# Eleven power matrices of a state-space scan: from VectorE, between the value steps, to GpSimd, in a row

## The chip, the cores and the metric

One core of a Trainium2 chip. The metric is the device time of one execution in microseconds (us). Three runs of the kernel before took 151.14, 151.69 and 152.08 us; the median is 151.69. The kernel has two parts that share the core, called A and B, and its output is their results side by side.

## The reference

Part A is a diagonal complex recurrence over 2,048 steps with 448 states, read in and out by complex matrices. Part B is attention of 16 heads in which each position looks at 8 positions, 2 apart.

```python
def _A_ref(x, Lambda_re, Lambda_im, B_re, B_im, C_re, C_im, log_dt, Dskip):
    ...
    Lam_bar = jnp.exp(dt * Lam)
    B_bar = ((Lam_bar - 1.0) / Lam)[:, None] * Bmat
    Bu = jnp.einsum("bld,pd->blp", x + 0j, B_bar)
    for t in range(L):
        h = Lam_bar[None, :] * h + Bu[:, t, :]
        hs.append(h)
    ...
    y = 2.0 * jnp.einsum("blp,dp->bld", hseq, Cmat).real + x * Dskip[None, None, :]

def _B_ref(x, wqkv, wo):
    ...
    idx = pos[:, None] - off[None, :]        # off = 0, 2, ..., 14
    logits = jnp.einsum("bhsd,bhswd->bhsw", q, kg) * scale
    attn = _softmax(jnp.where(mask[None, None, :, :], logits, -1e9), axis=-1)
    o = jnp.einsum("bhsw,bhswd->bhsd", attn, vg)
    return (...)(o, 0, 2, 1, 3).reshape(B, S, D) @ wo
```

## The kernel before

**Part B.** Projections (`proj_t`, `proj`) run on TensorE; VectorE multiplies queries with shifted keys (`qk`, L295 and L299), and TensorE sums these products into logits. `softmax` works on one half of each 16 positions at a time: `softmax(1)` the later half, `softmax(0)` the earlier one. It turns the logits (L330), takes their maxima on VectorE (L332), subtracts them on TensorE (L337), takes the exponential on ScalarE into a tile `e` (L339), sums on TensorE (L345), and normalises on VectorE (L348, L349). `pv` makes the values: for each of the 8 offsets VectorE multiplies weights by values (L389, 128x1792 bf16) and, from the second on, adds the product (L392, 128x1792). These are the value steps. There are four calls of `pv`: two for the later half, then two for the earlier one. A call's sum goes through a DMA transpose (L404), the output matrix on TensorE (L420), and out.

**Part A.** The recurrence is done in blocks. A power of the recurrence's factor acts on a block by a matrix product, so each power k has a "mat", a 128x1024 bf16 tile made by one multiplication of a pattern `Dm` with the power's rows of `Scat` (`mat`, L599). `Scat` is complete at about 15 us. There are thirteen: k = 1, 2, 3, 4, 8, 12, 16, 32, ..., 1024 (`KPOW`), and one more, `g`, of another shape. Who uses them:
- `level1` (L643, L647): blocks of four, with k = 1, in three groups of states, `mh` = 0, 1, 2.
- `scan` (L663 to L676): first k = 4, 8, 12, then seven steps with 16, 32, ..., 1024. Each step is a product on TensorE (L673) out of one of two buffers `pbuf`, and a copy on ScalarE (L676) into the other. The first 64 columns of these buffers must be zero; `alloc_h` clears them on GpSimd (L633).
- `ends` (L690, L692): the states G at the ends of the blocks, with k = 4, 8, 12.
- `correct` (L699, L700): with k = 1, 2, 3, a product of G on TensorE that VectorE adds to the other states (the corrections, 21 of them).
- `y` (L711 to L718): the output, sixteen pieces.

**Order.** The framework orders the instructions of each engine at build time: among those that are ready, the one emitted first goes first; after that an engine's queue is in order. Two kinds of edges are added by hand: `cx.chain` for TensorE, and `cx.order(ins, after, "NoSync")`, which puts an instruction behind another in its engine's order without a wait. `lanes` (projections) has GpSimd relays, memsets of one element (L130), whose last one is `cx.relay`; the last is done at 51.74 us. `alloc_h` puts its clearings behind it.

`mats_behind(keys, after)` makes mats and puts each behind the instruction `after`. In `body`, the mats of k = 1 and 4 go behind the maxima of the first softmax; the other eleven go through `put`, behind the value steps of the first two calls of `pv`, one or two to a gap. `pv` calls `between[w - 1]` behind its w-th addition. The same list holds the five steps of `softmax(0)`, named `fs`. `eng` in other functions chooses the engine of a copy.

The scan's buffers share memory with older tiles. `pbuf` of the first group uses the places of `e` and of the logits `lgs`, so their clearing has to wait until `softmax(0)` has read both.

Of the kernel before, what the change touches and what calls it, by code (L numbers as in the profile page):

```python
# [11 lines left out]
ALU = mybir.AluOpType  # L12
# [31 lines left out]
NPW = len(KPOW)  # L44
# [386 lines left out]
class PartA:  # L431
# [139 lines left out]
        for k in range(KT):  # L571
            nc.scalar.activation(self.Dg[:, k, :], ident[:], ACT.Copy, scale=dsk[:, k:k + 1])

    def mats_behind(self, keys, after):
        for i in keys:
            key = "g" if i == "g" else KPOW[i]
            self.cx.order(self.mat(key, self.Scat[:, NPW if i == "g" else i]), after, "NoSync")

    def rot_rows(self, re, im):
        V, Sg = self.nc.vector, self.Scat[:, NPW]  # L580
# [3 lines left out]
        V.tensor_scalar(Sg[PL:NCH, 1, 0:NM], re[PL:NCH], -1.0, None, op0=ALU.mult)  # L584
        return Sg

    def mat(self, key, scal):
        if key == "g":
            sh = [NCH, NM, 2, PL]
            t_ = self.pool.tile(sh, bf16, name="matg")  # L590
            in0 = self.Dm[:, :, 0].unsqueeze(1).unsqueeze(1).to_broadcast(sh)
            in1 = scal[:, :, 0:NM].rearrange("p h m -> p m h").unsqueeze(3).to_broadcast(sh)
            self.mats[key] = t_[:].rearrange("p m h q -> p m (h q)")
        else:
            sh = [NCH, 2, PL, MP]
            t_ = self.pool.tile(sh, bf16, name=f"mat{key}")
            in0, in1 = self.Dm[:].unsqueeze(1).to_broadcast(sh), scal.unsqueeze(2).to_broadcast(sh)
            self.mats[key] = t_[:].rearrange("p h q m -> p m (h q)")
        return self.nc.vector.tensor_tensor(t_[:], in0, in1, op=ALU.mult).ins  # L599

    def setup_b(self, eng):
        nc, cx = self.nc, self.cx
# [120 lines left out]
@with_exitstack  # L723
def body(ctx: ExitStack, tc: tile.TileContext, A_x, A_Lre, A_Lim, A_Bre, A_Bim, A_Cre, A_Cim, A_logdt, A_Dskip,
         B_x, B_wqkv, B_wo, out):
    nc = tc.nc
    pool = ctx.enter_context(tc.tile_pool(name="sb", bufs=1))
    psum = ctx.enter_context(tc.tile_pool(name="ps", bufs=1, space=bass.MemoryType.PSUM))
    out_v = out[0].rearrange("(p j) e -> p j e", j=T)
    cx = Ctx(tc, pool, psum)  # L730
    b = PartB(cx, B_x, B_wqkv, B_wo, out_v[:, :, D:2 * D])
    a = PartA(cx, A_x, A_Lre, A_Lim, A_Bre, A_Bim, A_Cre, A_Cim, A_logdt, A_Dskip, out[0].rearrange("(n b) e -> n b e", b=4)[:, :, 0:D])
    parts = ((512, 1024), (1024, 1536), (1536, 2048))
    b.alloc()
    b.load_xn(0, 2)
    b.load_w(D, 0, D, nc.scalar)
    a.load_params()
    b.load_xn(2, 4)
    cx.consts()
    a.consts()  # L740
    b.clear()
    nc.scalar.activation(cx.spot2[:], cx.wz[0:1, 0:1], ACT.Exp)
    b.load_w(0, D, D, nc.sync)
    for g in parts:
        b.load_x(*g)
    b.consts()
    b.load_w(2 * D, 2 * D, D, nc.sync)
    a.load_bc()
    a.load_x()
    b.zero_halo(b.vd)  # L750
    b.load_wo()
    a.load_c()
    a.load_d()
    cx.warm(8)
    turns = [lambda i=i: b.turn_x(i, "VA"[i % 2], ("pt", "lg")[i // 2]) for i in range(4)]
    for f in turns[:2]:
        for ins in f():
            cx.chain(ins)
    powers = a.params()
    cx.warm(2)  # L760

    def later():
        powers(b.turned)
        b.mix_w(a.reduced)
        a.params_g()
        return ()

    values = [b.proj(j, "A") for j in (*range(HJ, T), *range(HJ))]
    qk, soft = b.qk(0) + b.qk(1), {}
    weave = [(5, turns[2:] + [later])] + [(s_, [f]) for s_, f in zip(WEAVE, qk)]  # L770

    def turn():
        a.mats_behind(["g"], b.product)
        soft[1] = b.softmax(1)
        return soft[1][0][0]() + soft[1][0][1]()

    def prepare():
        a.mats_behind([0, 3], b.maxima)
        fs = mats_b[:1] + soft[1][0][4:] + mats_b[1:]
        return [ins for f in fs for ins in f()]  # L780

    mats_b = a.setup_b("A")
    weave += [(157, [turn])] + [(160 + 4 * i, [lambda i=i: soft[1][0][2 + i]()]) for i in range(2)] + [(200, [prepare])]
    cx.lanes([b.proj_t(t0, t1, g, "A") for t0, t1, gs in ((0, 256, (0, 1, 2)), (256, 512, (0, 1, 2)), (0, 512, (4, 5, 6, 3)))
              for g in gs]
             + [b.proj_t(*t, g, "A") for t in parts for g in (0, 1, 2, 4, 5, 6, 3)] + values, weave, 10)
    at1 = soft[1][1]
    b.halo(b.vd, 6, HALO)
    b.halo(b.vd, 0, 6)
    a.skip()  # L790
    fs, at0 = b.softmax(0)

    def put(*fs):
        return lambda after: [f() if callable(f) else a.mats_behind([f], after) for f in fs]

    wo = [b.pv(1, at1, 0, 4, between=[put(4, *fs[:2]), put(5, 6), put(*fs[2:4]), put(7, 8), put(fs[4]), put(9, 10)])]
    wo.append(b.pv(1, at1, 4, 8, between=[put(11, 12), put(), put(1, 2)]))
    a.alloc_h()
    for mh in range(3):
        a.level1(mh)  # L800
        a.scan(mh)
        if mh == 0:
            a.setup_c("A")
    wo[0]()
    for mh in range(3):
        a.ends(mh)
    for b_ in range(3):
        for mh in range(3):
            a.correct(b_, mh)
    wo[1]()  # L810
    wo.append(b.pv(0, at0, 0, 4))
    wo.append(b.pv(0, at0, 4, 8, True))
    for b_, r in itertools.product((3, 0, 1, 2), range(4)):
        ins = a.y(r, b_)
        if (b_, r) == (1, 3):
            wo[2]()
    turn, out = wo[3]
    cx.tail = None
    for i in ins[:8] + turn(0) + ins[8:] + turn(1):
        cx.chain(i)  # L820
    out()
# [31 lines left out]
```

## Time and profile before

One profiled execution of this kernel took 151.38 us; its span is 149.7 us.

| engine | busy, us | share of the span |
|---|---|---|
| TensorE, matmuls | 139.7 | 93% |
| VectorE | 131.5 | 88% |
| ScalarE | 90.7 | 61% |
| GpSimd | 8.7 | 6% |

What VectorE's time goes into, by line and shape (busy time, mean of one; then idle time before them):

```profile
L389 DVE TENSOR_TENSOR pvb<-attn,vd 128x1792 bf16<-128x1792 bf16 x31 | 32.8, 1080 | 0.0
L392 DVE TENSOR_TENSOR pvb<-pvb 128x1792 bf16<-128x1792 bf16 x27 | 29.2, 1081 | 0.0
L295 DVE TENSOR_TENSOR pr<-q,kT 128x3072 bf16<-128x3072 bf16 x16 | 27.9, 1755 | 1.4 <-PE lg L306 0.7 <-ACT q L144 0.6
L700 DVE TENSOR_TENSOR h<-co,h 128x512 bf16<-128x512 f32 x21 | 13.2, 685 | 2.0 <-PE gt L690 1.6 <-PE co L699 0.3
L599 DVE TENSOR_TENSOR mat<-Dm,Scat 128x1024 bf16<-128x1024 bf16 x13 | 8.4, 681 | 0.0
```

PE is TensorE, PEld its weight loads, DVE VectorE, ACT ScalarE, POOL GpSimd, SP SyncE. A duration covers an instruction's whole way through its engine; back to back, the next one starts a little earlier, so two value steps start 1.00 us apart and last 1.08. A busy TensorE is modelled: its matmuls are pipelined. The clock that TensorE was granted is full in the whole span. A wait is put down to the engine whose signal came last. In the kernel before, GpSimd does nothing after 74.75 us.

### The profile page before, as it was taken

What the parts mean: (1) busy time and instruction counts of PE and PEld (TensorE: products, weight loads), DVE (VectorE), ACT (ScalarE), POOL (GpSimd) and SP (SyncE); (2) the same over time, 40 slices, a digit from 0 to 9 for tenths busy, and PEclk for the clock granted to TensorE, in tenths of its full rate; (3) what the DMA queues carried; (4) which work ended last, traced back from release to release, by engine and by line L of the source; (5) the groups of instructions that cost most, each with busy time, mean ns of one, the idle gap of its engine ahead of it and who ended that gap; (6) DMA issues with size and microseconds to landing.
All of it is one profiled execution on the core that took longest, in us unless ns stands there. A gap on an engine that the chain in (4) does not pass through costs nothing.

```text
span 149.7 us, 3246 instructions
## 1 busy us (share of the span) xinstructions
PE 139.7 (93%) x1234; PEld 80.6 (54%) x1240; DVE 131.5 (88%) x178; ACT 90.7 (61%) x200; POOL 8.7 (6%) x84
## 2 busy tenths in 40 slices
PE   6999999999999999589999999999999999899790
PEld 2477744445665675245467555568565655445440
DVE  4368999998999859999999999995999999999821
ACT  3387947886754599964569967779421242245340
POOL 8110100000000200000000000000000000000000
PEclk9999999999999999999999999999999999999999
DMA  4999999993767706000004200045111121832121
GB/s 118 286 176 192 176 242 212 95 211 74 144 115 136 213 4 183 0 0 4 0 0 83 39 4 0 0 118 134 61 64 61 41 87 56 190 120 96 61 92 61
DMA packets 35534, 14.77 MB, mean 99 GB/s; under 512 B 27635, under 2 KB 35137, under 8 KB 35519
## 3 DMA queue, kind: packets, MB, share of 16 engines
q1 hardware_dynamic: 34954, 14.12, 44.2%
q10 hardware_dynamic: 565, 0.46, 0.9%
q8 instruction: 9, 0.15, 0.4%
q14 instruction: 6, 0.05, 0.2%
HBM read 3.85 MB, written 3.67 MB: 50 GB/s over the span
## 4 chain that ended last, share of the span: by engine, by line
PE 68%; DVE 18%; ACT 9%; issue 2%; DMA 1%; DVEq 0%; ACTq 0%
PE qk_ps L121 14%; PE l L643 13%; PE v_ps L121 8%; DVE pvb L392 8%; DVE pvb L389 7%; PE lg L306 6%; PE wo_ps L420 5%; PE warm L71 3%; PE y_ps L715 3%; PE l L647 3%; PE gt L690 3%; PE co L699 3%; ACT h L650 2%; PE l L673 2%; ACT Ccat L144 2%
## 5 line engine op out<-in xcount | busy, mean ns | idle before, releaser
L389 DVE TENSOR_TENSOR pvb<-attn,vd 128x1792 bf16<-128x1792 bf16 (+1 forms) x33 | 34.0, 1052 | 0.0
L643 PE MATMUL l<-xaT,Bcat 128*128 128x512 bf16 x108 | 29.5, 379 | 1.8 <-ACT h L650 1.6
L392 DVE TENSOR_TENSOR pvb<-pvb 128x1792 bf16<-128x1792 bf16 (+1 forms) x29 | 30.3, 1049 | 0.0
L295 DVE TENSOR_TENSOR pr<-q,kT 128x3072 bf16<-128x3072 bf16 x16 | 27.9, 1755 | 1.4 <-PE lg L306 0.7
L121 PE MATMUL qk_ps<-xbT,wqkv_nat 64*128 64x512 bf16 (+1 forms) x189 | 24.8, 353 | 0.1
L718 ACT CAST ya<-y_ps 128x448 bf16<-128x448 f32 x16 | 8.4, 533 | 18.7 <-PE y_ps L715 13.0
L715 PE MATMUL y_ps<-Ccat,h 128*128 128x448 bf16 x84 | 18.0, 353 | 0.0
L643 PEld LDWEIGHTS <-Bcat 128*128 128x128 bf16 x112 | 10.5, 99 | 10.7 <-issue 2.2
L121 PEld LDWEIGHTS <-wqkv_nat 64*128 64x128 bf16 x189 | 11.5, 94 | 8.7 <-issue 2.5
L420 PE MATMUL wo_ps<-wo_p,oT 128*128 128x448 bf16 x64 | 14.7, 352 | 1.0 <-DMA oT<-pvb 1.0
L650 ACT CAST h<-l 128x512 bf16<-128x512 f32 x21 | 12.4, 623 | 4.3 <-PE l L647 4.2
L700 DVE TENSOR_TENSOR h<-co,h 128x512 bf16<-128x512 f32 x21 | 13.2, 685 | 2.0 <-PE gt L690 1.6
L121 PE MATMUL v_ps<-wqkv_nat,xbT 64*128 64x448 bf16 x112 | 13.2, 360 | 0.0
L144 ACT CAST kT<-qk_ps 128x512 bf16<-128x512 f32 (+4 forms) x26 | 10.0, 424 | 3.7 <-PE qk_ps L121 3.6
L144 ACT CAST yb<-wo_ps 128x448 bf16<-128x448 f32 x14 | 7.5, 534 | 6.0 <-PE wo_ps L420 3.1
L144 ACT CAST q<-qk_ps 128x512 bf16<-128x512 f32 (+1 forms) x20 | 9.6, 497 | 1.2 <-PE qk_ps L121 1.1
L144 ACT CAST vd<-v_ps 128x448 bf16<-128x448 f32 x16 | 8.0, 539 | 4.0 <-PE v_ps L121 3.8
L715 PEld LDWEIGHTS <-h 128*128 128x128 bf16 x84 | 7.3, 98 | 5.3
L676 ACT CAST pbuf<-l 128x512 bf16<-128x512 f32 (+2 forms) x21 | 9.1, 439 | 1.5 <-PE l L673 1.5
L306 PE MATMUL lg<-pr,ones 128*32 128x256 bf16 x256 | 9.9, 275 | 0.0
L121 PEld LDWEIGHTS <-xbT 64*128 64x128 bf16 x112 | 7.6, 145 | 3.5 <-issue 1.9
L420 PEld LDWEIGHTS <-oT 128*128 128x128 bf16 x64 | 6.0, 98 | 6.5 <-DMA oT<-pvb 1.4
(137 smaller groups left out, 192.0 us busy)
## 6 DMA issues: line engine op xcount, KB each, us to landing
out_dram<-yb SPq DMA_DIRECT2D x16, 112.0 KB, 2.1
out_dram<-ya SPq DMA_DIRECT2D x16, 112.0 KB, 1.7
vd<-vd SPq DMA_DIRECT2D x1, 784.0 KB, 5.4
wqkv_nat<-in_B_wqkv_dram SPq DMA_DIRECT2D x2, 336.0 KB
vd<-vd SPq DMA_DIRECT2D x1, 588.0 KB
xn<-in_B_x_dram SPq DMA_DIRECT2D x2, 224.0 KB, 3.4
bX<-in_A_B_re_dram SPq DMA_DIRECT2D x1, 392.0 KB, 4.4
bX<-in_A_B_im_dram SPq DMA_DIRECT2D x1, 392.0 KB
```

Source lines behind the costliest of these rows:

```text
L121: ins = mm(g["ps"], lhsT=l_, rhs=r_, start=first, stop=not (g["left"][0] or g["left"][1]), skip_group_check=True).ins
L144: nc.scalar.copy(out, in_)
L295: queued(V.tensor_tensor(pr[:], q[0][:, :, n * qu:n * qu + n].unsqueeze(2).to_broadcast([KA, KT - 1, 4, n]), self.shifted(i, 0, KT - 1, s, ...
L306: out.append(mm(lg[32 * t:32 * t + 32, n * qu:n * qu + n], lhsT=l_, rhs=r_, start=not (s or qu or c), stop=(s == 1 and c == KT - 1), skip_ ...
L389: V.tensor_tensor(t_[:, c0:c1], at[:, w, jl0 + c0:jl0 + c1, :].unsqueeze(2).to_broadcast([NCH, c1 - c0, DH, H]), self.vd[:, off + c0:off + ...
L392: ins = V.tensor_tensor(acc[:, c0:c1], acc[:, c0:c1], t_[:, c0:c1], op=ALU.add).ins
L420: ins = nc.tensor.matmul(ps[:], lhsT=oT[:, 7 * i + 3 * odd + k, :], rhs=self.wo_p[:, odd, k, :], start=(k == 0), stop=(k == KT - 1)).ins
L643: nc.tensor.matmul(ps[:], lhsT=self.Bcat[:, k, m, :], rhs=self.xT[:, b, k, :], start=(k == 0), stop=(b == 0 and k == KT - 1))
L650: nc.scalar.copy(self.h[b][:, m, :], ps[:])
L676: nc.scalar.copy(dst[:, :, PAD:], ps[:])
L700: nc.vector.tensor_tensor(self.h[b][:, m, :], ps[:], self.h[b][:, m, :], op=ALU.add)
L715: out.append(nc.tensor.matmul(ps[:], lhsT=self.state(m, r, b), rhs=self.C[:, m, :], start=False, stop=(m == NM - 1), skip_group_check=True ...
```

## The change

The eleven mats that `put` placed between value steps are emitted at once, on GpSimd, behind the last relay, in the order k = 8, 12, 16, 32, ..., 1024, 2, 3. `mat` gets the engine as an argument; the mats of k = 1 and 4, and `g`, stay on VectorE. The steps of `softmax(0)` keep their places.

```diff
-    def mats_behind(self, keys, after):
+    def mats_behind(self, keys, after, eng=None):
         for i in keys:
             key = "g" if i == "g" else KPOW[i]
-            self.cx.order(self.mat(key, self.Scat[:, NPW if i == "g" else i]), after, "NoSync")
+            self.cx.order(self.mat(key, self.Scat[:, NPW if i == "g" else i], eng or self.nc.vector), after, "NoSync")
...
-    def mat(self, key, scal):
+    def mat(self, key, scal, eng):
...
-        return self.nc.vector.tensor_tensor(t_[:], in0, in1, op=ALU.mult).ins
+        return eng.tensor_tensor(t_[:], in0, in1, op=ALU.mult).ins
...
     def put(*fs):
-        return lambda after: [f() if callable(f) else a.mats_behind([f], after) for f in fs]
-
-    wo = [b.pv(1, at1, 0, 4, between=[put(4, *fs[:2]), put(5, 6), put(*fs[2:4]), put(7, 8), put(fs[4]), put(9, 10)])]
-    wo.append(b.pv(1, at1, 4, 8, between=[put(11, 12), put(), put(1, 2)]))
+        return lambda after: [f() for f in fs]
+
+    a.mats_behind([4, 5, *range(6, NPW), 1, 2], cx.relay, nc.gpsimd)
+    wo = [b.pv(1, at1, 0, 4, between=[put(*fs[:2]), put(), put(*fs[2:4]), put(), put(fs[4])])]
+    wo.append(b.pv(1, at1, 4, 8))
     a.alloc_h()
```

## The prediction

> **What bounds the kernel now.** I read the page's shares first, then the chain of waits, then VectorE's timeline around the edit, then GpSimd's. The shares and the chain:
>
> ```profile
> PE 139.7 (93%) x1234; PEld 80.6 (54%) x1240; DVE 131.5 (88%) x178; ACT 90.7 (61%) x200; POOL 8.7 (6%) x84
> PE 68%; DVE 18%; ACT 9%; issue 2%; DMA 1%; DVEq 0%; ACTq 0%
> ```
>
> The chain changes hands: up to 115.6 us it is mostly TensorE's, from there to 140.9 VectorE's, value step after value step. So the two are nearly level. How level shows in TensorE's waits after 56 us; the two late ones (0.96 us at 131.27, 0.87 us at 140.88) are all that it idles in the last stage before the tail:
>
> ```profile
> PE wo_ps L420 <- DMA oT<-pvb: 1.0, 1, 1.0
> PE pt_o L411 <- DVE pvb L392: 0.9, 1, 0.9
> ```
>
> VectorE's timeline where the mats lie, and where it meets the corrections (start, duration, operation, count; brackets hold idle time):
>
> ```profile
> 51.80 1.28 DVE L599 TENSOR_TENSOR mat<-Dm,Scat 128x1024 bf16<-128x1024 bf16 x2
> 54.81 0.96 DVE L348 RECIPROCAL rec<-den 128x128 bf16<-128x128 f32 x1 [1.73 <-PE den L345]
> ...
> 63.41 1.08 DVE L392 TENSOR_TENSOR pvb<-pvb 128x1792 bf16<-128x1792 bf16 x1
> 64.41 1.28 DVE L599 TENSOR_TENSOR mat<-Dm,Scat 128x1024 bf16<-128x1024 bf16 x2
> 65.62 1.08 DVE L392 TENSOR_TENSOR pvb<-pvb 128x1792 bf16<-128x1792 bf16 x1
> ...
> 73.64 0.67 DVE L349 TENSOR_TENSOR attn<-e,rec 128x1024 bf16<-128x1024 bf16 x1
> ...
> 101.90 1.08 DVE L389 TENSOR_TENSOR pvb<-attn,vd 128x1792 bf16<-128x1792 bf16 x1
> 104.57 1.29 DVE L700 TENSOR_TENSOR h<-co,h 128x512 bf16<-128x512 f32 x2 [1.59 <-PE gt L690]
> ```
>
> From 55.9 to 103.0 VectorE never idles. Two mats take 1.21 us from start to start (64.41 to 65.62): 0.60 each.
>
> **What leaves VectorE.** Eleven mats by 0.60: 6.6 us. TensorE's work stays what it is. If nothing else changed, VectorE would be 6.6 us early, but TensorE would still give G at 104.4 (the first correction matmul), and after it could only save its two waits, 1.8 us. That is the ceiling of the gain.
>
> **What lands on GpSimd: the length of one mat.** No two-input operation of GpSimd is in the trace. The nearest rows are its one-input selects: 128 elements in 293 ns, 32 in 203 ns, so 0.93 ns an element behind a fixed 0.17 us. With 1,024 elements and one stream that is 1.1 us, the low end; two input streams taken in turn give 0.17 + 2 x 0.95 = 2.1 us; a third turn for the output 3.0 us, the high end. I take 2.1, since the select too writes what it reads and pays once for both. [...]
>
> **What GpSimd and VectorE do to each other.** The one place where a reading GpSimd operation meets a two-input VectorE operation is at the start:
>
> ```profile
> 1.41 0.29 POOL L61 TENSOR_SCALAR_AFFINE_SELECT nident<-nident 128x128 bf16<-128x128 bf16 x1
> 2.37 0.62 DVE L498 TENSOR_TENSOR Dm<-ident 128x512 bf16<-128x512 bf16 x1
> 2.71 0.47 POOL L370 TENSOR_SCALAR_AFFINE_SELECT maskw<-maskw 16x128 bf16<-16x128 bf16 x1
> ```
>
> The select at 2.71 has 128 elements like that at 1.41, yet takes 0.18 us longer, and ends 0.19 us after VectorE's operation ends at 2.99. That is what waiting for the other's read would look like (its pattern differs too, so it is a hint, no proof). A port that one of two waits for must make the other wait in turn once the first has it. Memsets, which only write, lengthen nothing (the one at 74.44 lies in a value step of the usual 1.08 us). The bounds for VectorE are therefore nothing, and the whole 2.1 us for each mat; I take the whole, by the select's row. [...]
>
> **The sum.** GpSimd can start at 51.75, after its last relay. VectorE's operations and the mats then alternate: a mat, an operation, a mat. The holds are 11 x 2.1 = 23.1 us. Hidden is what VectorE spends idle or on operations without two SBUF inputs: 1.73 waiting for den, reciprocals 0.96 and 0.87, the dsk cast 0.12, two maxima at 0.60: 4.9 us. Less the 6.6 removed, VectorE is 23.1 - 4.9 - 6.6 = 11.6 us late when the row is done, near 84 us.
>
> GpSimd's own queue matters too. It is in order, and behind the relay stand the clearings of the scan's buffers:
>
> ```profile
> 51.47 0.27 POOL L130 MEMSET spot<- 1x1 f32 x2 [1.11 <-PE v_ps L121]
> 51.68 0.52 POOL L633 MEMSET pbuf<- 128x128 bf16 x4
> 52.13 0.14 POOL L635 MEMSET G<- 128x7 bf16 x1
> 57.22 0.31 POOL L633 MEMSET pbuf<- 128x256 bf16 x1 [4.95 <-ACT Bcat L144]
> 74.44 0.31 POOL L633 MEMSET pbuf<- 128x256 bf16 x1 [16.91 <-PE l L647]
> ```
>
> The mats are emitted before these and are ready, so I expect all eleven ahead of them. The last one clears a buffer in the place of softmax weights e, which the product at 73.64 frees at 74.31; the scan's first step, at 78.38, needs it. That product has five mats less in front of it (3.0 us) and the unhidden holds (18.2 us): freed at 89.5, cleared at 89.8, the scan 11.4 us late, and G at 104.4 + 11.4 = 115.8. The mats themselves are in time: the third (power 16) is made by about 60 and wanted at 78, the ninth (power 1024) by about 79 and wanted at 86.4 even before. The maxima that TensorE waits for at 59.3 and the dsk cast that ScalarE's Dg copies and all its copies behind wait for come late as well, by less than 11.4 us, so they add nothing.
>
> VectorE's order is made at build time by what is ready. Seven value steps of the last pair already stand ahead of the corrections (between 94.89 and 102.98) because the builder saw VectorE free there; with 6.6 us less planned on VectorE I expect six more, 6.0 us. The corrections then start at 102.98 + 11.6 + 6.0 = 120.6, not 104.57: 16.0 us late. Behind them TensorE's y products set the end and lose the 1.8 us of waits: +14.2 us. Without the six moved steps the corrections would start with G, and the end be 11.4 late.
>
> The profiled execution took 151.38 us, 149.7 of it span; 151.38 + 14.2 = 165.6. It lies 0.3 under the median shown, which is inside the 0.9 that the three runs spread over. I round to 165.5. No queue of DMAs is moved; the output transfers on SyncE only stand behind a later transpose of pvb (L404), already counted.
>
> **Rivals.**
> - *No exclusion* (not slower): both engines run side by side. For it: relays and clearings beside VectorE's work lengthen nothing, and the select's pattern may explain its 0.18 us. Eleven mats end at 51.75 + 11 x 2.15 = 75.4, the clearings 1.2 later at 76.6, before 78.38. VectorE gains 6.6, the end at most 1.8: 149.6 to 151.4. It holds up to 2.3 us a mat ((78.38 - 1.2 - 51.75) / 11); a longer one delays the scan by the queue alone, by 7.6 us at 3.0. Chance 0.20.
> - *A cheap hold*: mats of the low end, 1.1 us, or a port that is shared within an instruction. 12.1 - 4.9 - 6.6 = 0.6 late, plus six moved steps: corrections 5.0 late, the end 3.2: 152 to 155. For it: a second input that costs no turn of its own is all that 1.1 us needs. Chance 0.12.
> - *GpSimd starves*: value steps start 1.00 apart and last 1.08, so they may hand the port on among themselves. GpSimd then gets in beside maxima and reciprocals alone, some six mats; five are left until VectorE waits for G, near 107, and the clearings behind them until 118, 40 us after 78.38: about 190. Against it: the select got its turn at once. Chance 0.10.
>
> **Numbers.** The forecast has 0.58, with 160 to 172 of its own (2.1 us may be 1.8 to 2.5; moved steps or not). A measurement here tells about 1%, 1.5 us, from no change. Range 150.0 to 172: it takes in the cheap hold and most of the first rival, and leaves out starving and mats near 3.0 us (175). Faster by over 1% needs under 150.2, the better half of the first rival: 0.09. Within 1%: its other half, 0.11. Slower: 0.80.
>
> **What would show it.** Mats of about 2.1 us start to start on GpSimd where VectorE idles, 3.1 where it multiplies; value steps between 56 and 84 us that start 3 us apart in place of 1.00; the last clearing of pbuf near 90; the corrections' wait for G gone, and VectorE waited for instead. It is wrong if value steps keep 1.00 us beside the mats, if the clearings stand ahead of the row, or if the corrections start near 105.

## The result and the profile after

The changed kernel takes 161.53 us, the median of four runs (161.45 to 161.78); the kernel before takes 151.41 beside it (151.09 to 152.08). The ratio is 1.0665, with a 95% interval of 1.0623 to 1.0708: slower by 6.7%. The profiled execution took 161.45 us, 159.6 of it span, so it stands against the 151.38 and 149.7 of before: 10.1 us more. In one experiment below, the one that moves the value steps back, two of the four executions were slow ones: its ratio is over the other two, and its trace is of a slow one (162.44 us).

The shares of the profile's page and the chain of waits:

```profile
PE 141.0 (88%) x1240; PEld 81.1 (51%) x1240; DVE 140.9 (88%) x167; ACT 90.7 (57%) x200; POOL 36.4 (23%) x95
PE 69%; DVE 21%; DMA 4%; issue 3%; ACT 2%; DVEq 0%; ACTq 0%
```

VectorE has eleven instructions less (167, not 178) and yet 9.4 us more busy time. What the page counts as busy includes standing still inside an instruction: a value step beside the row counts 2.78 us, one behind it 1.08. GpSimd's timeline behind its relays, then VectorE's in the same stretch (start, duration, operation, count; brackets hold idle time):

```profile
51.29 27.73 POOL L599 TENSOR_TENSOR mat<-Dm,Scat 128x1024 bf16<-128x1024 bf16 x11
...
84.50 0.31 POOL L633 MEMSET pbuf<- 128x256 bf16 x1 [4.70 <-DVE attn L349]
```

```profile
51.38 4.66 DVE L599 TENSOR_TENSOR mat<-Dm,Scat 128x1024 bf16<-128x1024 bf16 x2
55.96 0.94 DVE L348 RECIPROCAL rec<-den 128x128 bf16<-128x128 f32 x1
...
77.19 2.78 DVE L392 TENSOR_TENSOR pvb<-pvb 128x1792 bf16<-128x1792 bf16 x1
79.89 1.08 DVE L389 TENSOR_TENSOR pvb<-attn,vd 128x1792 bf16<-128x1792 bf16 x1
...
117.38 13.31 DVE L700 TENSOR_TENSOR h<-co,h 128x512 bf16<-128x512 f32 x21
```

Beside the row a value step lasts 2.78 us and the next starts 2.70 after it (77.19 to 79.89); the first step behind the row's end (51.29 + 27.73 = 79.0) lasts the usual 1.08. So each mat costs the value step beside it 1.70 us; this is called the hold below. VectorE's own mats of k = 1 and 4 pay it too: 4.66 us for two that took 1.28. The reciprocal, with one input, keeps its length (0.94 us, 0.96 before). The corrections now start at 117.38 without a wait, where VectorE waited 1.59 us and began at 104.57.

TensorE's waits after 56 us (total, times, longest), which before held nothing over 1.6:

```profile
PE lt L337 <- DVE mx L332: 4.2, 2, 3.1
PE wo_ps L420 <- DMA oT<-pvb: 3.5, 1, 3.5
PE l L673 <- ACT pbuf L668: 3.1, 1, 3.1
```

And its clock behind the second of these, at 93.5 us (stretch, length, busy time and count, granted clock, DMA share, GB/s):

```profile
92.00:94.00 2.00, 0.48 (x2) 0.95 0.51 93
94.00:96.00 2.00, 2.00 (x9) 0.50 0.00 0
96.00:98.00 2.00, 2.00 (x11) 0.70 0.00 0
```

TensorE waits for VectorE's maxima, for the scan's buffers and for transposed values, and runs some 4 us at a lower clock. The scan's first step and the first output product, in the kernel before and then in the changed one, from TensorE's timelines:

```profile
78.38 0.44 PE L673 MATMUL l<-pbuf,mat 128*128 128x128 bf16 x4 [0.15 <-ACT pbuf L668]
95.32 0.54 PE L420 MATMUL wo_ps<-wo_p,oT 128*128 128x448 bf16 x2
```

```profile
85.20 0.43 PE L673 MATMUL l<-pbuf,mat 128*128 128x128 bf16 x4 [3.06 <-ACT pbuf L668]
93.52 0.36 PE L420 MATMUL wo_ps<-wo_p,oT 128*128 128x448 bf16 x1 [3.49 <-DMA oT<-pvb]
```

TensorE's order has changed too. Before, the first output product stands behind all seven steps of the first scan (the last is at 86.41); in the changed kernel the builder has put one such product between the fourth step (89.19) and the fifth (94.49). G, the first correction matmul, comes at 115.96 us, not at 104.4.

### The profile page after: what moved, and what is told of

Read it like the earlier page. It is cut to its first block, busy times and chain, and to the rows that moved or that the text cites. A ratio compares the mean times of both kernels' runs of the same rounds, so it can differ in the third digit from the quotient of the medians.

```text
span 159.6 us, 3253 instructions
## 1 busy us (share of the span) xinstructions
PE 141.0 (88%) x1240; PEld 81.1 (51%) x1240; DVE 140.9 (88%) x167; ACT 90.7 (57%) x200; POOL 36.4 (23%) x95
## 4 chain that ended last, share of the span: by engine, by line
PE 69%; DVE 21%; DMA 4%; issue 3%; ACT 2%; DVEq 0%; ACTq 0%
PE qk_ps L121 14%; PE y_ps L715 13%; DVE pvb L389 7%; PE wo_ps L420 7%; PE l L643 7%; PE v_ps L121 6%; DVE pvb L392 5%; PE lg L306 5%; PE co L699 3%; DVE mat L599 3%; PE l L673 3%; PE warm L71 3%; PE gt L690 3%; DMA oT<-pvb 3%; PE y_ps L711 2%
## 5 line engine op out<-in xcount | busy, mean ns | idle before, releaser
L389 DVE TENSOR_TENSOR pvb<-attn,vd 128x1792 bf16<-128x1792 bf16 (+1 forms) x33 | 41.9, 1286 | 0.0
L392 DVE TENSOR_TENSOR pvb<-pvb 128x1792 bf16<-128x1792 bf16 (+1 forms) x29 | 34.7, 1199 | 0.0
L643 PE MATMUL l<-xaT,Bcat 128*128 128x512 bf16 x112 | 31.2, 389 | 0.0
L599 POOL TENSOR_TENSOR mat<-Dm,Scat 128x1024 bf16<-128x1024 bf16 x11 | 27.7, 2556 | 0.0
L420 PE MATMUL wo_ps<-wo_p,oT 128*128 128x448 bf16 x64 | 14.8, 352 | 3.5 <-DMA oT<-pvb 3.5
L130 POOL MEMSET spot<- 1x1 f32 x45 | 4.1, 91 | 43.1 <-PE qk_ps L121 23.8
L700 DVE TENSOR_TENSOR h<-co,h 128x512 bf16<-128x512 f32 x21 | 13.1, 683 | 0.2
L420 PEld LDWEIGHTS <-oT 128*128 128x128 bf16 x64 | 6.0, 98 | 9.4 <-DMA oT<-pvb 4.0
```

Source lines behind the costliest of these rows:

```text
L389: V.tensor_tensor(t_[:, c0:c1], at[:, w, jl0 + c0:jl0 + c1, :].unsqueeze(2).to_broadcast([NCH, c1 - c0, DH, H]), self.vd[:, off + c0:off + ...
L392: ins = V.tensor_tensor(acc[:, c0:c1], acc[:, c0:c1], t_[:, c0:c1], op=ALU.add).ins
L420: ins = nc.tensor.matmul(ps[:], lhsT=oT[:, 7 * i + 3 * odd + k, :], rhs=self.wo_p[:, odd, k, :], start=(k == 0), stop=(k == KT - 1)).ins
L599: return eng.tensor_tensor(t_[:], in0, in1, op=ALU.mult).ins
L643: nc.tensor.matmul(ps[:], lhsT=self.Bcat[:, k, m, :], rhs=self.xT[:, b, k, :], start=(k == 0), stop=(b == 0 and k == KT - 1))
L700: nc.vector.tensor_tensor(self.h[b][:, m, :], ps[:], self.h[b][:, m, :], op=ALU.add)
```

## Experiments

Three questions: does GpSimd's reading hold VectorE up, or GpSimd's work of any kind, or the new order of work? By which route does VectorE's lateness reach the end? How many mats can GpSimd take, and where? Each ratio is to the kernel before on the same chip, with its 95% interval.

### The row without reading

The eleven mats on GpSimd become memsets; the order of work on the other engines stays that of the changed kernel. The mats' values are left out.

```diff
-        return eng.tensor_tensor(t_[:], in0, in1, op=ALU.mult).ins
+        return (eng.memset(t_[:], 0.0) if eng is self.nc.gpsimd else eng.tensor_tensor(t_[:], in0, in1, op=ALU.mult)).ins
```

> The changed kernel, but GpSimd fills each of the eleven tiles with zeros by one memset instead of multiplying: it writes as much and reads nothing; the eleven matrices are left out of the result. The order on every other engine is the same as in the changed kernel. Theory X (a GpSimd operation that reads and a VectorE operation with two inputs in the on-chip memory take turns at one port): value steps start 1.00 us apart from 56 us on, the weights of the earlier half are normalised at about 71, the scan's first step is at 77 to 79, and the time is 149.5 to 152. Rival B (any work of GpSimd slows VectorE): value steps beside the row stay over 1.5 us apart. Rival O (the new build order is what costs): value steps at 1.00 but the time stays above 156.

148.75 us, ratio 0.9843 (0.982 to 0.9867), 0.75 us under the range expected. GpSimd's row and VectorE's steps beside and behind it, from the timelines of this kernel:

```profile
51.30 9.83 POOL L599 MEMSET mat<- 128x1024 bf16 x11
```

```profile
56.22 2.09 DVE L389 TENSOR_TENSOR pvb<-attn,vd 128x1792 bf16<-128x1792 bf16 x2
...
65.44 1.08 DVE L389 TENSOR_TENSOR pvb<-attn,vd 128x1792 bf16<-128x1792 bf16 x1
...
104.08 1.29 DVE L700 TENSOR_TENSOR h<-co,h 128x512 bf16<-128x512 f32 x2 [1.08 <-PE gt L690]
```

With nothing read, every value step is back at 1.00 us from start to start, beside the row (56.22) as behind it, and VectorE waits for G again. Same instructions elsewhere, same order: the reading costs 10.1 + 2.2 = 12.3 us, each kernel taken against the kernel before that ran beside it. Neither GpSimd's work as such nor the new order does it alone: here too an output product stands between the fourth and the fifth step of the scan, at 82.56, and it waits for nothing. The value step that starts at 79.89 in the changed kernel starts at 65.44 here, so the row costs VectorE 14.4 us. The run also gives the ceiling: with the mats for nothing the kernel gains 2.2 us (150.93 to 148.75).

### The row with one input

GpSimd copies in place of multiplying; the multiplication is left out.

```diff
-        return eng.tensor_tensor(t_[:], in0, in1, op=ALU.mult).ins
+        return (eng.tensor_copy(t_[:], in0) if eng is self.nc.gpsimd else eng.tensor_tensor(t_[:], in0, in1, op=ALU.mult)).ins
```

> The changed kernel, but each of the eleven tiles is a copy of the pattern Dm by GpSimd: one input in place of two; the multiplication by the powers is left out. Theory X: reading is what counts, so VectorE's value steps still take turns with the row, each held by the shorter operation: 1.8 to 2.1 us from step to step where the changed kernel shows 2.70, a row of 18 to 22 us in place of 27.7, and a time of 152 to 157. Rival (only GpSimd operations with two inputs exclude VectorE): steps at 1.00, time 149.5 to 152.

152.81 us, ratio 1.0115 (1.0068 to 1.0163). The row takes 17.40 us, and VectorE's timeline near its end (69.0) shows the hold:

```profile
68.07 1.92 DVE L389 TENSOR_TENSOR pvb<-attn,vd 128x1792 bf16<-128x1792 bf16 x1
```

The step beside the end of the row lasts 1.92 us, 0.84 more than the usual 1.08, and the next, at 69.92, is back at 1.08. One input held for 0.84 us and two for 1.70: twice the reading came with twice the hold.

### Mats beside the corrections

In the kernel before, the mats of k = 2 and 3 go to GpSimd behind the first correction. `"Sync"` makes GpSimd wait for that correction. L700 is VectorE's largest two-input operation with one input outside SBUF, the on-chip memory (`co` lies in PSUM, the accumulators).

```diff
+            ins = nc.vector.tensor_tensor(self.h[b][:, m, :], ps[:], self.h[b][:, m, :], op=ALU.add).ins; (b, m) == (0, 0) and self.mats_behind([1, 2], ins, nc.gpsimd, "Sync")
...
-    wo.append(b.pv(1, at1, 4, 8, between=[put(11, 12), put(), put(1, 2)]))
+    wo.append(b.pv(1, at1, 4, 8, between=[put(11, 12)]))
```

> The kernel before, but the mats of 2 and 3 are made by GpSimd behind the first correction, beside VectorE's corrections, which read one input from the accumulators (PSUM) and one from the on-chip memory. Theory X (only operations with two inputs in the on-chip memory take turns with GpSimd's reads): the corrections keep 0.69 us and start 0.60 to 0.64 apart, a mat takes 1.7 to 1.9 us, and the time is 0 to 1.2 us below before. Rival B2 (any VectorE operation that reads the on-chip memory takes turns): two corrections are held by 1.7 us each and the time is 1 to 3.5 us above.

150.35 us, ratio 0.9925 (0.9895 to 0.9955). The lines of the two operations (shortest, median and longest in ns, first and last start):

```profile
L599 POOL TENSOR_TENSOR mat<-Dm,Scat x2: 1897/1898/1898, 105.3 to 107.1; 128x1024 bf16<-128x1024 bf16 x2
```

```profile
L700 DVE TENSOR_TENSOR h<-co,h x21: 678/682/693, 104.5 to 117.2; 128x512 bf16<-128x512 f32 x21
```

Neither lengthens the other: 21 corrections between 678 and 693 ns, and both mats at 1.90 us, as long as the first mat of the changed kernel's row, which had nothing ahead of it (1.899, the shortest of the eleven). So it is not enough that both engines work and that GpSimd reads: with one of VectorE's two inputs in PSUM, neither was held.

### Closing the routes, one by one

At the row's end VectorE is 14.4 us later than in the run without reading. The next kernels keep the row and take away one way in which that reaches TensorE.

The scan's buffers no longer reuse the place of the softmax weights:

```diff
-        self.pbuf = [[pool.tile([NCH, m1 - m0, PAD + NCH], bf16, name=f"pbuf{m0}{i}", tag=f"pbuf{m0}{i}" if m0 else ("e", "lgs")[i]) for i in range(2)]
+        self.pbuf = [[pool.tile([NCH, m1 - m0, PAD + NCH], bf16, name=f"pbuf{m0}{i}", tag=f"pbuf{m0}{i}") for i in range(2)]
```

> The changed kernel, but the first group's scan buffers have a place of their own instead of that of e and of the logits, so their clearing waits for nothing of VectorE. The order on TensorE, VectorE and ScalarE is unchanged. Theory X with three limits nearly level: the scan's first step comes 3 us earlier, at about 82, but TensorE still waits for the transposed values near 93 and the corrections still for VectorE near 117, so the time is 160.3 to 161.7. Rival Q (the reused buffer is what carries the loss to TensorE): the 3 us come through, 158 to 159.

162.36 us, ratio 1.0747 (1.0712 to 1.0782): no gain. The scan starts at 83.15, 2.05 us earlier than in the changed kernel, but TensorE's queue then stops at the same product, from its timeline:

```profile
93.92 0.56 PE L420 MATMUL wo_ps<-wo_p,oT 128*128 128x448 bf16 x1 [5.94 <-DMA oT<-pvb]
```

The wait that was 3.49 us is 5.94, and the product starts 0.4 us later than it did. What the buffers gave back, the values took.

Then the other way round: the output products of L420 for the first call of `pv` stand behind the first scan's last step, where they stood before the change, and the buffers are as they were.

```diff
-        def out():
+        def out(behind=None):
...
-                    if last:
-                        cx.chain(ins)
+                    if last or behind:
+                        cx.chain(ins) if last else cx.order(ins, behind, "NoSync")
...
-                nc.tensor.matmul(ps[:, m - m0, :], lhsT=M[T << s_][:, m, :],
+                self.step = nc.tensor.matmul(ps[:, m - m0, :], lhsT=M[T << s_][:, m, :],
...
-            a.setup_c("A")
-    wo[0]()
+            behind = a.step; a.setup_c("A")
+    wo[0](behind)
```

> The changed kernel, but the first output products of part B (L420) are put behind the last step of the first scan in TensorE's order, so that TensorE doesn't wait for the transposed values at 89.4 to 93.5 us. VectorE's order is unchanged. Theory X: G comes 4 to 5 us earlier, near 111, with no stretch at a granted clock of 0.7, but VectorE still reaches the corrections at about 117, so the time falls by 0 to 1.5: 160 to 161.6. Rival O (TensorE's order and its cold clock are what costs): 155 to 158.

163.12 us, ratio 1.0804 (1.0777 to 1.0832): the wait at 93 us is gone and nothing is won. The scan still starts at 85.42, TensorE waits 2.73 us for it and runs at a clock of 0.60 between 84 and 88 us, and later TensorE waits 2.69 us for the first corrections, whose start VectorE sets at 117.60. Both single edits came out above the ranges expected (162.36 against at most 161.7, 163.12 against at most 161.6).

Both edits together:

> The changed kernel with both reliefs of TensorE at once: scan buffers of their own, and part B's first output products behind the first scan. VectorE's order is unchanged. If VectorE's late arrival at the corrections (117.4 to 117.8 us in the changed kernel and in both single reliefs) sets the end, G is ready 6 us before it, TensorE idles and the time stays at 161 to 163.5. If the two waits of TensorE stand in for each other and are the cause together, it falls to 155 to 158.

162.83 us, ratio 1.0756 (1.0707 to 1.0805). The scan now starts at 82.27, and a third route opens. From the timelines of TensorE, ScalarE and SyncE's DMA queue:

```profile
109.41 0.27 PE L673 MATMUL l<-pbuf,mat 128*128 128x128 bf16 x1 [4.71 <-ACT pbuf L676]
```

```profile
108.66 0.53 ACT L144 CAST yb<-wo_ps 128x448 bf16<-128x448 f32 x1 [4.96 <-DMA out_dram<-yb]
```

```profile
89.43 16.52 SPq L404 DMA_TRANSPOSE oT<-pvb  x2
106.04 15.59 SPq L426 DMA_DIRECT2D out_dram<-yb  x8
```

Read from the bottom: on SyncE's queue the output transfers stand behind a second transpose of values that come late; the transposes end at 105.95, the transfers begin at 106.04. So the two buffers yb are not sent; ScalarE, which has a third product to write there, stands still for 4.96 us with the scan's copies behind it; TensorE waits for one of those copies and then runs at a clock of 0.50 (108 to 112 us).

The same kernel with the value steps that the builder had moved ahead of the corrections put back behind them, all but the seven that stood there before. `late` does it for both kinds of step: it counts them from where `behind`, the last correction, is set, and orders each beyond the seventh behind it, without a semaphore.

```diff
-                    ins = V.tensor_tensor(acc[:, c0:c1], acc[:, c0:c1], t_[:, c0:c1], op=ALU.add).ins
+                    ins = self.late(V.tensor_tensor(acc[:, c0:c1], acc[:, c0:c1], t_[:, c0:c1], op=ALU.add).ins)
...
-    wo[1]()
+    wo[1](); b.behind = a.fixed
```

> As the kernel with both reliefs of TensorE, and the value steps of the last pair that the builder moved ahead of the corrections are put behind them again: seven ahead, as before the change. Theory: VectorE reaches the corrections 6 to 7 us earlier, at 110.5 to 111.5, and the end moves until VectorE's total work binds again, which leaves its own loss to the port: 156.5 to 159. If the moved steps don't matter: 161 to 163.5, as without this edit.

Ratio 1.0617 (1.0525 to 1.0709); the two executions behind it took 159.62 and 161.89 us. That is above the 156.5 to 159 expected, and not clear of the changed kernel's 1.0665 (1.0623 to 1.0708). In the trace VectorE ends its steps at 110.77, 6.6 us earlier than in the kernel with both edits (117.35), and then waits 5.38 us for TensorE, which has waited 4.35 us for ScalarE's copy of the scan: the third route still holds it. And that kernel with four yb buffers in place of two:

```diff
-                yb = pool.tile([NCH, D], bf16, name="yb", tag="yb", bufs=2)
+                yb = pool.tile([NCH, D], bf16, name="yb", tag="yb", bufs=4)
```

> As the kernel with both reliefs and the value steps put back, and four buffers in place of two for part B's output pieces (yb). In that kernel the output transfers stood on SyncE's queue behind the second transpose of values, which waits for VectorE's steps until 104; ScalarE waited 4.6 us for a buffer, TensorE for ScalarE, and G came at 115.7 once more. Theory (every way from the late value steps to TensorE costs the same 5 to 6 us, and the three were in each other's shadow): with the last way open, G comes near 110, the corrections start at 110 to 112, and what is left is VectorE's own loss, 156.5 to 159. If still another wait takes its place: 160 to 162.5.

156.80 us, ratio 1.0358 (1.0291 to 1.0425): 4.7 us under the changed kernel. VectorE's timeline shows the corrections without a wait:

```profile
110.91 13.10 DVE L700 TENSOR_TENSOR h<-co,h 128x512 bf16<-128x512 f32 x21
```

That is 6.3 us later than before (104.57); VectorE is busy 93.8 of the 94 us from 53 to 147. Ahead of the corrections it does the seven value steps of before and no more. What is left, 156.80 - 151.31 = 5.5 us, is by this trace VectorE's own loss.

### Fewer mats, other places

Two mats (k = 8 and 12) on GpSimd behind the relay, the other nine where they were; then five (8, 12, 16, 32, 64):

```diff
-    a.mats_behind([4, 5, *range(6, NPW), 1, 2], cx.relay, nc.gpsimd)
+    a.mats_behind([4, 5], cx.relay, nc.gpsimd)
```

> Only the mats of 8 and 12 on GpSimd, behind the last relay; the other nine on VectorE between the value steps as before the change. Theory X: they take turns with VectorE's mats of 1 and 4 from 51.3 to 55.5, mostly in the 1.73 us in which VectorE waited for den; the reciprocal starts 0.5 to 1.5 late, and 1.2 is saved later: 150.3 to 152. A cost in proportion to the count (10.1 us for eleven) would give 152.8.

> The mats of 8, 12, 16, 32 and 64 on GpSimd, the other six on VectorE as before the change. Theory X, from the changed kernel's trace: VectorE is 5.5 us late when the fifth mat is done (near 63), 3.0 is saved, and most of the rest is on the path: 152 to 154.5, value steps at 1.00 again after 63. In proportion to the count: 155.5.

Two: 150.03 us, ratio 0.9911 (0.9879 to 0.9942), 0.3 us under the range expected. Five: 154.05 us, ratio 1.0152 (1.011 to 1.0194). The two mats meet VectorE's own two and the 1.73 us in which it waited for den: the reciprocal starts at 55.90, not 54.81, 1.1 us late, and two mats of 0.60 have left VectorE. The other three meet the product L349 and two value steps, which together last 3.9 us longer. So 2, 5 and 11 mats cost -1.4, +2.6 and +10.1 us.

The idle time can serve VectorE itself. In the kernel before, its own mats of k = 8 and 12 move there, next to those of 1 and 4:

```diff
-        a.mats_behind([0, 3], b.maxima)
+        a.mats_behind([0, 3, 4, 5], b.maxima)
```

> The kernel before with one edit and nothing on GpSimd: the mats of 8 and 12 are made by VectorE behind the maxima with those of 1 and 4, where it waits 1.73 us for den, instead of between value steps. Theory (1.2 us of VectorE's work moves into idle time; the row of memsets showed that eleven mats less are worth 2.2 us at the end): 0.3 to 1.3 us faster than before. Rival (TensorE binds all the way, VectorE's 1.2 us are worth nothing): within 0.3 of before.

149.96 us, ratio 0.9919 (0.989 to 0.9948). VectorE's timeline:

```profile
51.43 2.49 DVE L599 TENSOR_TENSOR mat<-Dm,Scat 128x1024 bf16<-128x1024 bf16 x4
54.44 0.96 DVE L348 RECIPROCAL rec<-den 128x128 bf16<-128x128 f32 x1 [0.52 <-PE den L345]
```

Four mats fit, and 0.52 us of the wait is left. With the two beside the corrections as well:

> Both of the last two edits on the kernel before: the mats of 8 and 12 in VectorE's idle time, those of 2 and 3 on GpSimd beside the corrections. Theory: 2.4 us less for VectorE between value steps and no turns taken: 0.5 to 2 us faster than before, 149 to 150.4. If either edit is worth nothing, as the better of the two alone.

149.62 us, ratio 0.9906 (0.9877 to 0.9936). It is the fastest kernel here that computes everything, 1.8 us under the kernel before. Its interval overlaps those of its two parts, so whether they add is open.

## Why the prediction held, and where its sum was off

**The mechanism: right.** In these runs a GpSimd operation that reads SBUF and a VectorE operation with two SBUF inputs took turns, one for one: beside the eleven mats of the row VectorE did eleven operations with two SBUF inputs (two mats, the product L349, eight value steps), and a value step there lasted up to 2.78 us, not 1.08. Three runs show it from three sides: eleven copies held value steps too, by up to 0.84 us; beside eleven memsets, which read nothing, value steps kept 1.00 us from step to step; and the corrections, with one input in PSUM, kept 682 ns beside mats of 1.90 us. The traces show the turns, not what enforces them: that it is a port was the author's reading. The rivals of no exclusion and of a starving GpSimd fall: value steps did not keep 1.00 us, and the row ended at 79.0, GpSimd getting its turn after each step. The cheap hold falls with the hold measured.

**One mat on GpSimd: 2.1 us forecast, 1.90 measured** (beside the corrections). Of the three readings that of two input streams in turn came nearest, too dear by a tenth. No run shows the 2.15 us that the first rival counts for a mat.

**What VectorE pays: the term that was mis-sized.** The forecast let a mat hold VectorE for its whole length, 2.1 us, with value steps 3 us apart. No run shows such a hold: the steps were 2.70 apart, a hold of 1.70, less even than the mat's own 1.90. Eleven holds make 18.7, not 23.1. The sum also counts VectorE's operations without two SBUF inputs as not held. The trace of before does not show that, but the changed kernel's does: beside the row the reciprocal took 0.94 us (0.96 before), the two maxima 0.68 each and the cast 0.15, as before, all with their one input in PSUM. So the time that hides part of the holds was about right: 18.7 - 14.4 = 4.3 us, against 4.9. So unhidden holds were 14.4, not 18.2 us. VectorE ended its steps ahead of the corrections at 117.38 against 102.98 before, by coincidence 14.4 us later as well; less seven moved steps of 1.00, its own lateness was 7.4 us and not 11.6. (14.4 - 6.6 is 7.8; the execution profiled after the change was 0.4 us ahead when the row began, 51.38 against 51.80.)

**The clearings: right in order and in what they wait for, too late by 5 us.** They did stand behind the row, and that cost nothing: the last one was free to go at 79.8 and waited 4.70 us for VectorE's product of e, as the forecast's other half said. The product freed the buffer at 84.4, not 89.5: the holds were 3.8 us less (18.2 - 14.4), one value step fewer stands ahead of it in the new order (eleven, not twelve, so 1.0 us), and the execution was 0.4 ahead. The scan began 6.8 us late (85.20 against 78.38), not 11.4. The clearing was not even the last that the scan waited for: ScalarE's copy into the same buffer (L668), freed by the same product, ran from 84.47 to 85.06, the clearing from 84.50 to 84.81.

**G: 115.96 us, forecast 115.8, by another sum.** G is 11.6 us late, and the scan only 6.8. The rest came from a place that the forecast did not look at. It expected VectorE's order to change at build time, not TensorE's; but an output product now stands inside the first scan, and it waited 3.49 us at 93.52 for values that came late. In the kernel before no output product waits ahead of G. The lower clock behind that wait (0.95, 0.50 and 0.70 in three stretches of 2 us) cost 0.05 x 2 + 0.50 x 2 + 0.30 x 2 = 1.7, an estimate. 6.8 + 3.5 + 1.7 = 12.0; the kernel before was idle for 0.4 us in short gaps between the scan's start and G (25.59 us busy of 25.99), the changed one for next to nothing beside the wait, and 12.0 - 0.4 = 11.6. The maxima and the cast added nothing, as forecast: TensorE stood still for the scan's buffers long after them. That the total met the forecast is chance.

**The moved steps: right in number, wrong in what they cost.** Seven value steps moved ahead of the corrections, six were forecast. The corrections began at 117.38, 12.8 us late, against 120.6 and 16.0. But the forecast took their start for what sets the end (16.0 - 1.8 = 14.2), and it did not: behind the first correction matmul TensorE has output products to do, eight of them from 116.40 to 118.08 us in the changed kernel, and it did not idle while VectorE was 1.2 us behind G's 11.6.

**The end.** It follows TensorE from G on. 11.56 late there, less the two waits of 0.96 and 0.87 that were forecast to go and went, is 9.7; the last transposes of the values (L411) start 9.93 us later than before (150.81 against 140.88), and the execution took 10.1 more. TensorE sets the end, as forecast: VectorE finished at 146.9 and waited 4.54 us for it. So of the forecast's 14.2, 11.4 - 1.8 = 9.6 was met, by the chance that G was, and the 4.6 us that it put on top for the moved steps did not come. (For the case without moved steps the forecast wrote "11.4 late"; it left out there the 1.8 that it subtracts everywhere else.) The ceiling of 1.8 was a little low: the run of memsets gained 2.2.

**The ways into TensorE's queue.** The forecast followed one, the reused buffer. It passed over the output product in TensorE's in-order queue, and held the transposes on SyncE ahead of the output transfers for counted. Each stood in the shadow of another, so that closing one or two gave nothing (162.36, 163.12, 162.83 us) and moving the steps back as well gave nothing clear of the noise; with all of them closed 4.7 us came back. Four yb buffers alone in the changed kernel were not tried, nor the return of the steps alone, so how the 4.7 us divide among the edits is open.

## What to carry to other kernels

Work taken off VectorE for GpSimd was not free here while VectorE ran operations with two SBUF inputs: each 1.90 us mat cost 1.70 us there to save 0.60. So look first for a stage in which VectorE has an input in PSUM (beside mats the corrections kept 682 ns, the reciprocal 0.94 us) or is idle. When a producer is late, list all its consumers in in-order queues before one of them is mended; one mended wait only uncovers the next. Look for idle time on the full engine itself too: two mats moved into VectorE's 1.73 us gave as much (1.5 us) as two on GpSimd (1.4).

## What the runs showed of the hardware

- A mat takes 1.90 us beside the corrections and a value step 1.00 from start to start, but in turns the period is 2.70 and not 2.90; 0.20 us of the mat overlaps the step. A row of 1,024-element memsets takes 0.89 us each (9.83 / 11), and a copy's hold is 0.84 us, half of the two-input 1.70.
- TensorE's granted clock fell to half in or behind waits of 3 to 6 us, for about 4 us: with that of 3.49 (0.50 at 94 to 96 us and 0.70 at 96 to 98 of the changed kernel), of 5.94 (0.50 at 94 to 98 with the scan's own buffers), of 4.71 (0.50 at 108 to 112 with both edits). It was not strict. The wait for the maxima, 3.15 us up to 64.4 in the changed kernel, was followed by a clock of 1.00 there; the same wait, again 3.15 us, was followed by 0.69 (64 to 66) and 0.73 (66 to 70) in the kernel with all routes closed. A wait of 3.06 us in the changed kernel was followed by 1.00; with the products moved, one of 2.73 was followed by 0.60 (84 to 88) and one of 2.69 by 0.62 (118 to 122). What makes the clock fall in one case and not in another, these runs do not show. By the estimate above the wait of 3.49 us cost 1.7 us more than its length; the four executions of the changed kernel had mean clocks of 0.966 to 0.986.
- With both edits ScalarE stood still 4.96 us for an output transfer, and the cause was a transpose ahead of it in SyncE's queue (it ended at 105.95, the transfers began at 106.04): what the DMA queue held back showed as ScalarE's idle time.
